# Scores of an attention block in two-half and three-half stages, with the third half in the banks of the feed-forward layer

## Chip, cores, metric

One core of one Trainium2 chip. The metric is the device time of one execution in microseconds, as the median of several; kernels are compared by the ratio of the mean time of one kernel's fast runs to that of the other's fast runs of the same rounds, so a ratio is not quite the ratio of the medians quoted beside it. TensorE is written PE in the profile, VectorE DVE, ScalarE ACT, GpSimd POOL, SyncE (which issues most transfers) SP.

## The reference

Attention with a local window of 96 keys and 8 global keys and a distance bias for each head, followed by a feed-forward layer with softplus:

```python
scores = q @ k.T / sqrt(D) - slope[h] * dist      # 4 x 8 heads, 768 rows, D = 64
a      = softmax(where(is_global | is_local, scores, -1e9))
x      = (a @ v) laid out as 3072 x 512
out    = softplus(x @ w_in) @ w_out               # 512 -> 2048 -> 512
```

## The kernel before

The rows are cut into 24 blocks of 128 (six to a batch entry), two blocks make a window, and there are 12 groups of 256 rows for the feed-forward layer. A half is four of a block's eight heads, and a stage is one run of score matmuls on TensorE. A planner inside the kernel starts each operation in a simulated order and the instructions are issued in that order, engine by engine. TensorE interleaves mm1 (x @ w_in), mm2 (softplus @ w_out), the scores and pv (a @ v).

```python
raw = tile_pool(bufs=2); qkv = tile_pool(bufs=2)           # q32, qb, qT ... two buffers each
s_ps = [psum [P, 8, P]] * 2     # one half (4 heads) of a block's scores each: two banks each
h_ps = [psum [P, 512]] * 2      # the two banks of mm1
x_ps, o_ps                      # one bank each: pv and mm2
...
def scores_both(n):             # a stage: both halves of block n
    scores(n, 0, s_ps[0], True)
    scores(n, 1, s_ps[1], True)
...
def globals_k(n):               # GpSimd: global keys over rows of the previous block's keys, in place
def globals_v(n): ...           # VectorE: the same for v
...
pl = Planner({"S0": 1, "S1": 1, "X": 1, "H": 2, "O": 1, ..., "qb": 2, "kb": 2, "qT": 2}, ...)
...
for i in range(2):              # a window's q and k are transposed by two DMAs each
    o = pl.add(f"D{what}{w}", "sp", 1.3, ..., takes=takes if i == 0 else (), ...)
...
frees_q = [(first_t[w, "q"], "qT")] if half == 1 and n % 2 == 1 else []   # after the window's last scores
```

`takes=takes if i == 0 else ()`: in the plan only the first of the two transposes has to wait for a free buffer of transposed q.

The softmax here doesn't subtract the row's maximum and nothing guards it: scores larger than these inputs give would overflow.

## Time and profile before

| | before |
|---|---|
| median of three runs | 218.81 us (218.69 to 219.37) |
| span of the profiled run | 217.1 us |
| PE, ACT, DVE, POOL busy | 97%, 72%, 53%, 28% |
| mean granted TensorE clock | 0.999 |

PE is the engine to watch: in the chain of waits it carries 86% of the span, and the other engines wait for it. The row of the page with the granted clock, in 40 slices, is 9 everywhere (9 means 90% or more):

```profile
PEclk9999999999999999999999999999999999999999
```

### The profile page before, as it was taken

To read this page: it belongs to the slowest core of one execution; us is meant where nothing else is said; L and a number is where in the kernel's file an instruction comes from. 1 tells how busy PE (TensorE), PEld (TensorE's weight loads), DVE (VectorE), ACT (ScalarE), POOL (GpSimd) and SP (SyncE) were. 2 spreads that over 40 slices of the span, in tenths; PEclk is the share of its full clock that TensorE was granted. 3 is DMA by queue.
4 is the path that set the end of the run, shared out by engine and by line. 5 is a ranking of instruction groups with operands and counts; after the bars stand their busy time and mean duration, and the time that the engine had idled before them with its cause. 6 is when DMAs were issued, how large, how long until landed. Compare 5 with 4: busy or idle time off the path is not lost.

```text
span 217.1 us, 5087 instructions
## 1 busy us (share of the span) xinstructions
PE 210.4 (97%) x2073; PEld 146.2 (67%) x2073; DVE 115.8 (53%) x247; ACT 157.1 (72%) x210; POOL 61.1 (28%) x119
## 2 busy tenths in 40 slices
PE   7799999999999999999999999999999999999993
PEld 7577775766667766667767767666766766776542
DVE  6565554728696585885544954663763663110120
ACT  4686885995969957888959669668768758857700
POOL 3770290014727170540404260331350000000000
PEclk9999999999999999999999999999999999999999
DMA  5999999999999986969866885887791211201112
GB/s 159 301 220 196 271 154 197 222 303 278 176 264 262 211 192 195 259 86 227 133 167 174 163 184 167 198 195 195 158 209 48 76 24 51 72 0 48 51 44 102
DMA packets 71511, 35.98 MB, mean 166 GB/s; under 512 B 27328, under 2 KB 68544, under 8 KB 71488
## 3 DMA queue, kind: packets, MB, share of 16 engines
q1 hardware_dynamic: 67120, 31.27, 63.0%
q0 software_dynamic: 4224, 4.19, 12.2%
q8 instruction: 16, 0.26, 0.5%
q10 hardware_dynamic: 144, 0.20, 0.2%
q14 instruction: 7, 0.06, 0.1%
HBM read 27.26 MB, written 6.29 MB: 155 GB/s over the span
## 4 chain that ended last, share of the span: by engine, by line
PE 86%; DMA 9%; POOL 2%; ACT 1%; SPq 0%; issue 0%; DVE 0%; ACTq 0%
PE h_ps L492 36%; PE o_ps L520 31%; PE s_ps L393 5%; DMA w_in_bf<-in_moe_w_in_dram 4%; PE x_ps L448 4%; PE s_ps L545 3%; DMA q<-in_q_dram 2%; DMA v<-in_v_dram 2%; PE s_ps L520 2%; PE o_ps L646 1%; PE h_ps L319 1%; PE s_ps L378 1%; POOL vb L302 1%; ACT pb L434 1%; PE h_ps L470 1%; PE x_ps L445 1%
## 5 line engine op out<-in xcount | busy, mean ns | idle before, releaser
L492 PE MATMUL h_ps<-XT,w_in_bf 128*128 128x256 bf16 x768 | 96.4, 273 | 0.5 <-DMA w_in_bf<-in_moe_w_in_dram 0.3
L492 PEld LDWEIGHTS <-w_in_bf 128*128 128x128 bf16 x768 | 73.2, 98 | 21.1 <-DMA w_in_bf<-in_moe_w_in_dram 0.8
L520 PE MATMUL o_ps<-w_out_bf,g 128*128 128x512 bf16 x320 | 82.2, 379 | 0.0
L503 ACT ACTIVATE e<-h_ps 128x512 f32<-128x512 f32 x96 | 59.2, 630 | 29.8 <-PE h_ps L492 29.5
L511 ACT ACTIVATE g<-e 128x1024 bf16<-128x1024 f32 x48 | 50.7, 1056 | 0.8
L520 PEld LDWEIGHTS <-g 128*128 128x128 bf16 x352 | 31.9, 98 | 23.8 <-issue 0.3
L430 ACT ACTIVATE pb<-z 128x1024 bf16<-128x1024 f32 (+1 forms) x40 | 39.1, 985 | 8.2 <-DVE z L424 8.0
L424 DVE TENSOR_TENSOR z<-s_ps,biasA 128x1024 f32<-128x1024 f32 x34 | 40.8, 1219 | 7.1 <-PE s_ps L393 6.5
L302 POOL CAST vb<-v 64x512 bf16<-64x512 f32 (+1 forms) x46 | 27.5, 598 | 13.2 <-DMA v<-in_v_dram 11.2
L459 DVE RECIPROCAL rcp<-x_ps 128x4 f32<-128x4 f32 x44 | 7.9, 180 | 43.0 <-PE x_ps L448 38.9
L302 POOL CAST kb<-k 64x512 bf16<-64x512 f32 x32 | 19.7, 615 | 35.8 <-DMA k<-in_k_dram 34.6
L564 DVE COPY osb<-o_ps 128x512 f32<-128x512 f32 x20 | 13.7, 686 | 25.7 <-PE o_ps L520 25.5
L460 DVE TENSOR_TENSOR xs<-x_ps,rcp 128x256 bf16<-128x256 f32 x44 | 18.7, 425 | 1.5
L448 PEld LDWEIGHTS <-pb 128*128 128x128 bf16 x320 | 14.5, 97 | 4.1
L393 PEld LDWEIGHTS <-kT 64*128 64x128 bf16 x352 | 10.0, 94 | 8.4 <-issue 7.2
L393 PE MATMUL s_ps<-qT,kT 64*128 64x128 bf16 x352 | 15.1, 218 | 0.0
L448 PE MATMUL x_ps<-vb,pb 128*128 128x65 bf16 x288 | 14.6, 193 | 0.0
L362 POOL COPY kT<-kT 128x32 bf16<-128x32 bf16 x16 | 3.3, 209 | 39.2 <-issue 19.8
L371 DVE COPY vb<-vb 4x512 bf16<-4x512 bf16 x32 | 9.9, 309 | 0.5
L293 DVE CAST qb<-q 128x1024 bf16<-128x1024 f32 x10 | 6.9, 690 | 5.2 <-DMA q<-in_q_dram 5.1
L646 PE MATMUL o_ps<-zeros 128*128 128x128 bf16 x89 | 7.8, 251 | 1.0 <-DVE zeros L599 1.0
L434 ACT ACTIVATE pb<-s_ps 128x1024 bf16<-128x1024 f32 (+1 forms) x8 | 7.3, 917 | 1.6 <-PE s_ps L393 1.6
(61 smaller groups left out, 99.3 us busy)
## 6 DMA issues: line engine op xcount, KB each, us to landing
out_dram<-osb SPq DMA_DIRECT2D x23, 256.0 KB, 2.3
q<-in_q_dram SPq DMA_DIRECT2D x11, 512.0 KB, 5.4
k<-in_k_dram SPq DMA_DIRECT2D x11, 512.0 KB, 5.8
v<-in_v_dram SPq DMA_DIRECT2D x11, 512.0 KB, 5.4
w_in_bf<-in_moe_w_in_dram POOLq DMA_DIRECT2D x4, 512.0 KB, 8.1
w_out_bf<-in_moe_w_out_dram POOLq DMA_DIRECT2D x4, 512.0 KB, 11.0
q<-in_q_dram SPq DMA_DIRECT2D x2, 256.0 KB, 4.1
k<-in_k_dram SPq DMA_DIRECT2D x2, 256.0 KB, 4.4
```

The costliest lines, as they stand in the source:

```text
L302: copy_on[eng](dst[64 * r : 64 * r + 64, hs, :], src)
L393: nc.tensor.matmul(s_t[:, 4 * sub + (lh // 2 if i == 0 else 2 * (lh // 2) + b), :], k_of(n - b, rows, m), q_of(n, rows, m), start=begin, s ...
L424: nc.vector.tensor_tensor(packed(n, z), rows_of(n, s_t), bias, ALU.add)
L430: nc.scalar.activation(pb[:, 0:nr, :], z[:, 0:nr, :], AF.Exp, scale=1.0 / root_d)
L448: nc.tensor.matmul(xv[:, lh, :], pb[:, 2 * j + b, :], vb_of(n - b)[:, h, :], start=b == 0, stop=b == 1,)
L460: nc.vector.tensor_tensor(xs[:, 4 * half : 4 * half + 4, :], xv[:, :, 0:D], rcp[:][:, :, None].to_broadcast([P, 4, D]), ALU.mult,)
L492: nc.tensor.matmul(hv[:, j, :], w_in_bf[:, m, fb * P : fb * P + P], XT[:, m, W * g : W * g + W], start=(m == 0), stop=(m == NM - 1),)
L503: nc.scalar.activation(e[:, p % 2, :].rearrange("p (a t r) -> p a r t", a=4, r=2), state["h", g, p][:].rearrange("p (a r t) -> p a r t", a ...
L511: nc.scalar.activation(gt[:, 4 * c : 4 * c + 4, :].rearrange("p a t -> p (a t)"), state["e", g, c][:].rearrange("p a t -> p (a t)"), AF.Ln ...
L520: nc.tensor.matmul(dst, state["g", g][:, fb, ns * P : ns * P + P], w_out_bf[:, fb, :], start=(fb == 0), stop=(fb == NFB - 1),)
L564: copy_on[eng](osb[:], src)
L646: nc.tensor.matmul(o_ps[:, 0:P], zeros[:], zeros[:])
```

## The change

Intent: a stage of scores has a fixed cost on TensorE (about 0.21 us in the profile of before, worked out in the prediction below), so put three halves in a stage instead of two, from block 12 on. In the program's layout no pair of banks is free for the third half, so it takes both mm1 banks while the stage lasts. Since a block's first half now runs together with the block before it, the global keys can't overwrite the older block's keys in place yet; a shifted copy (kp) is used instead.

```diff
+    def stage(items, slot, off):
+        for j, (n, half) in enumerate(items):
+            s_t = (h_ps, s_ps[0], s_ps[1])[j]
+            ...
+                    takes=(("S0",), ("S1",), ("H",), ("H",)) if j == 0 else (),
+    def attention_triple(n):
+        stage([(n, 0), (n, 1), (n + 1, 0)], ...)
+        stage([(n + 1, 1), (n + 2, 0), (n + 2, 1)], ...)
...
+    def global_keys(n, rank, half=None, copied=False):
+        ...
+        for h in range(2):
+            if half in (None, h):
+                gk[n, h] = op = pl.add(f"gk{n}", "pool", dur, fn, rank, after=after)
...
+    def copy_k(n, half):        # GpSimd: keys of the previous block to kp, global keys on top
...
+        if isinstance(s_t, list):   # bias from the two mm1 banks: two instructions
```

Uncut, it also gives the new operations tuned places (a table of offsets), offers loads of windows from 6 on earlier, and orders mm2 from group 5 on differently.

More of the change, by code (lines that the diff above doesn't have):

```diff
@@ L14 @@
 BF16 = mybir.dt.bfloat16
+OFF = (-27.07, 2.51, 30.33, 25.71, -15.87, 17.77, -14.25, 0.3, 10.38, -16.15, 14.93, 41.55,
+       10.74, -48.65, -23.68, -19.66, 40.71, 6.61, -15.76, 29.51, 1.83, 2.96, -0.96, -3.56, -12.08)
 class Op:
@@ L354, in vb_of, with globals_k @@
         return vb_ring[n // 2 % NRING][:, n % 2, :, :]
-    def globals_k(n):
+    def globals_k(n, ms=slice(0, NPAIR)):
         first = n - n % NBLK
-        kd = state["kT", (n - 1) // 2][:, (n - 1) % 2, :, :]
-        ks = state["kT", first // 2][:, 0, :, :]
+        kd = state["kT", (n - 1) // 2][:, (n - 1) % 2, ms, :]
+        ks = state["kT", first // 2][:, 0, ms, :]
         nc.gpsimd.tensor_copy(
@@ L393, in scores @@
                 nc.tensor.matmul(
-                    s_t[:, 4 * sub + (lh // 2 if i == 0 else 2 * (lh // 2) + b), :],
-                    k_of(n - b, rows, m),
+                    part_of(s_t, 4 * sub + (lh // 2 if i == 0 else 2 * (lh // 2) + b)),
+                    prev_k(n, half, rows, m) if b else k_of(n, rows, m),
                     q_of(n, rows, m),
@@ L399, in scores, with part_of, prev_k @@
                 )
+    def part_of(s_t, j):
+        if isinstance(s_t, list):
+            return s_t[j // 4][:, P * (j % 4) : P * (j % 4) + P]
+        return s_t[:, j, :]
+    def prev_k(n, half, rows, m):
+        if ("kp", n, half) in state:
+            return state["kp", n, half][rows, m - 2 * half, :]
+        return k_of(n - 1, rows, m)
+    def copy_k(n, half):
+        first = n - n % NBLK
+        kp = tile_of(work, ("kp", n, half), [P, 2, P], BF16)
+        ms = slice(2 * half, 2 * half + 2)
+        nc.gpsimd.tensor_copy(kp[:], state["kT", (n - 1) // 2][:, (n - 1) % 2, ms, :])
+        nc.gpsimd.tensor_copy(
+            kp[:].rearrange("p m (r t) -> p m r t", r=2)[:, :, :, 0:GH],
+            state["kT", first // 2][:, 0, ms, :].rearrange("p m (r t) -> p m r t", r=2)[:, :, :, 0:GH],
+        )
     def rows_of(n, t):
@@ L423, in add_bias @@
             bias = bias.rearrange("p (e j) t -> p e j t", e=2)
+        if isinstance(s_t, list):
+            nr = 2 if n % NBLK == 0 else 4
+            bias = bias0 if n % NBLK == 0 else biasA
+            for e, bank in enumerate(s_t):
+                part = slice(nr * e, nr * e + nr)
+                nc.vector.tensor_tensor(
+                    z[:, part, :], bank[:, 0 : nr * P].rearrange("p (j t) -> p j t", t=P),
+                    bias[:, half, part, :], ALU.add,
+                )
+            return
         nc.vector.tensor_tensor(packed(n, z), rows_of(n, s_t), bias, ALU.add)
@@ L659 @@
     whole = ((ALL, range(NPAIR)),)
+    TRIPLES = 12
+    LATE = 5
+    STAGES = {12: ((4, 5), (5, 2)), 15: ((6, 1), (6, 6)), 18: ((7, 5), (8, 2)), 21: ((9, 1), (9, 6))}
     POOL_ORDER = "q1 in0 in1 out0 q2 out1 in2 in3 out2 out3".split()
@@ L724 @@
     for w in range(4, NWIN):
-        load_rest(w, base(2 * w) - 13.87)
+        load_rest(w, base(2 * w) - 13.87 - (3.0 if 2 * w >= TRIPLES else 0.0))
     for gate, w, what in gates:
@@ L737, in attention_window @@
     def attention_window(w):
-        u = base(2 * w)
+        u = base(2 * w) - (3.0 if 2 * w >= TRIPLES else 0.0)
         last = 1 if w == 0 else 0
@@ L772, in attention_window @@
                         lambda op, what=what, hs=hs: cast(op.on, w, what, hs),
-                        u - (7.94 if w < T_DMA else 5.33) + 0.1 * (what == "k"),
+                        u - (7.94 if w < T_DMA else 5.33 if 2 * w < TRIPLES else OFF[24]) + 0.1 * (what == "k"),
                         after=loaded[w, what] if w else [loaded[w, what][part]],
@@ L934, in attention_block, with attention_values @@
             )
-    for w in range(NWIN):
-        attention_window(w)
-        for n in (2 * w, 2 * w + 1):
-            attention_block(n)
+    def attention_values(n, half, rank):
+        i, w = n % NBLK, n // 2
+        prev = n - 1 if i > 0 else None
+        po = pl.add(
+            f"pv{n}{half}", "pe", 0.13 if i == 0 else 0.25, lambda op: pv(n, half, x_of(op)), rank,
+            after=[exps[n, half], *v_of(w, half), gv.get(n),
+                   *(v_of(prev // 2, half) if prev is not None else ())],
+            takes=(("X",),), frees=[(exps[n, half], "pb")], behind=[pvs.get((n, 0))],
+        )
+        no = pl.add(
+            f"norm{n}{half}", "dve", 0.62, lambda op: normalize(n, half, x_of(po)), rank + 0.1,
+            after=[po], behind=[norm.get((n, 0))], takes=(("xs",),) if half == 0 else (),
+            frees=[(po, "X")],
+        )
+        pvs[n, half], norm[n, half] = po, no
+        if half:
+            xdone[n] = pl.add(
+                f"DX{n}", "sp", 1.3, lambda op: x_dma(n), base(n) - 19.37,
+                after=[norm[n, 0], no], frees=[(norm[n, 0], "xs")], dma=(32, 27), slack=1.7,
+            )
@@ new lines, in global_keys @@
+    def global_keys(n, rank, half=None, copied=False):
+        first = n - n % NBLK
+        after = [*outs[first // 2, "k", 0], *outs[(n - 1) // 2, "k", 0]]
+        if copied:
+            fn, dur = lambda op: copy_k(n, half), 0.6
+        else:
+            ms = slice(0, NPAIR) if half is None else slice(2 * half, 2 * half + 2)
+            fn, dur = lambda op: globals_k(n, ms), 0.22
+            after += [score[n - 1, h] for h in range(2) if half in (None, h)]
+        for h in range(2):
+            if half in (None, h):
+                gk[n, h] = op = pl.add(f"gk{n}", "pool", dur, fn, rank, after=after)
@@ new lines, in global_values @@
+    def global_values(n, rank):
+        gv[n] = pl.add(
+            f"gv{n}", "dve", 0.68, lambda op: globals_v(n), rank,
+            after=[pvs[n - 1, 1], *casts[n - n % NBLK >> 1, "v"]],
+        )
+    def stage(items, slot, off):
+        group = None
+        for j, (n, half) in enumerate(items):
+            i, w = n % NBLK, n // 2
+            s_t = (h_ps, s_ps[0], s_ps[1])[j]
+            after = [*outs[w, "q", 0], *outs[w, "k", 0], gk.get((n, half))]
+            if i > 0:
+                after += outs[(n - 1) // 2, "k", 0]
+            ops = [
+                pl.add(
+                    f"scores{n}{half}", "pe", (0.19 if j == 0 else 0.0) + (0.12 if i == 0 else 0.225),
+                    lambda op, n=n, half=half, s_t=s_t: scores(n, half, s_t, True),
+                    slot if j == 0 else -900.0, after=after, behind=[group],
+                    takes=(("S0",), ("S1",), ("H",), ("H",)) if j == 0 else (),
+                    frees=[(first_t[w, "q"], "qT")] if half == 1 and n % 2 == 1 else [],
+                )
+            ]
+            if j == 0:
+                head = ops[0]
+            group = score[n, half] = ops[0]
+            need.append((head, after))
+            ab = pl.add(
+                f"bias{n}{half}", "dve", (0.7 if i == 0 else 1.22) + (0.15 if j == 0 else 0.0),
+                lambda op, n=n, half=half, s_t=s_t: add_bias(n, half, s_t),
+                slot + off[j], after=[group], takes=(("z",),),
+                frees=[(head, ("H", "S0", "S1")[j])],
+            )
+            exps[n, half] = pl.add(
+                f"exp{n}{half}", "act", 0.6 if i == 0 else 1.05,
+                lambda op, n=n, half=half: expo(n, half), slot + off[3 + j],
+                after=[ab], takes=(("pb",),), frees=[(ab, "z")],
+            )
+        return head
@@ new lines, in attention_triple @@
+    def attention_triple(n):
+        (ga, pa), (gb, pb) = STAGES[n]
+        a, b = NSLOT * ga + pa, NSLOT * gb + pb
+        if n % NBLK:
+            global_keys(n, a - 4.0)
+            global_values(n, base(n - 1) + 5.38)
+            global_keys(n + 1, a - 4.0, 0, True)
+        need.clear()
+        before_mm1[ga, pa] = head = stage([(n, 0), (n, 1), (n + 1, 0)], a - 0.6, OFF[0:6])
+        wait_all(head)
+        if n % NBLK:
+            global_keys(n + 1, a + 1.0, 1)
+        global_keys(n + 2, a + 1.1, 0)
+        global_keys(n + 2, a + 1.2, 1, True)
+        attention_values(n, 0, a + OFF[12])
+        attention_values(n, 1, a + OFF[13])
+        if n % NBLK:
+            global_values(n + 1, a + OFF[18])
+        attention_values(n + 1, 0, a + OFF[14])
+        need.clear()
+        before_mm1[gb, pb] = head = stage([(n + 1, 1), (n + 2, 0), (n + 2, 1)], b - 0.6, OFF[6:12])
+        wait_all(head)
+        attention_values(n + 1, 1, b + OFF[15])
+        global_values(n + 2, b + OFF[19])
+        attention_values(n + 2, 0, b + OFF[16])
+        attention_values(n + 2, 1, b + OFF[17])
@@ new lines, in wait_all @@
+    def wait_all(head):
+        for _, ops in need:
+            for o in ops:
+                if o is not None and o is not head and o not in head.after:
+                    head.wait_for(o)
+    need, before_mm1 = [], {}
+    for w in range(NWIN):
+        if 2 * w < TRIPLES:
+            attention_window(w)
+            for n in (2 * w, 2 * w + 1):
+                attention_block(n)
+        elif 2 * w % 3 == 0:
+            attention_window(w)
+            attention_window(w + 1)
+            attention_triple(2 * w)
+            attention_window(w + 2)
+            attention_triple(2 * w + 3)
@@ L947 @@
                 after=[xdone[2 * g], xdone[2 * g + 1], landed_in[p * NS // NSLOT]],
-                takes=(("H",),),
+                behind=[before_mm1.get((g, p))], takes=(("H",),),
             )
             ex = pl.add(
-                f"sexp{g}_{p}", "act", 0.59, lambda op, g=g, p=p: softplus_exp(g, p), r + 0.5,
+                f"sexp{g}_{p}", "act", 0.59, lambda op, g=g, p=p: softplus_exp(g, p), r + (0.5 if g < LATE else OFF[20]),
                 after=[m1], takes=(("e",),) if p % 2 == 0 else (), frees=[(m1, "H")],
@@ L956 @@
                     f"sln{g}_{p // 2}", "act", 1.06,
-                    lambda op, g=g, p=p: softplus_ln(g, p // 2), r + 0.9, after=[ex, prev_ex],
+                    lambda op, g=g, p=p: softplus_ln(g, p // 2), r + (0.9 if g < LATE else OFF[21]), after=[ex, prev_ex],
                     takes=(("g",),) if p == 1 else (), frees=[(prev_ex, "e")],
@@ L969 @@
                         1000.0 + 4 * part + chunk,
-                        after=[lns[g, chunk], before],
+                        after=[lns[g, chunk]], behind=[before],
                         takes=((LAST[part][2][0],),) if chunk == 0 else (),
@@ L991 @@
                 lambda op, g=g, ns=ns, c=c: mm2_one(g, o_ps[:], ns, range(4 * c, 4 * c + 4)),
-                NSLOT * (g + 1) + p + (-2.58 if g < 4 else 0.5),
-                after=[lns[g, c], landed_out[c], mm2s.get((g, p - 1))],
+                NSLOT * (g + 1) + p + (-2.58 if g < 4 else OFF[22] if g >= LATE else 0.5),
+                after=[lns[g, c], landed_out[c], mm2s.get((g, p - 1)) if g < 3 else None],
+                behind=[mm2s.get((g, p - 1)) if g >= 3 else None],
                 takes=(("O",),) if c == 0 else (),
@@ L1003 @@
                 ),
-                r - 2.06 + 4 * ns, after=[mm2s[g, last], copies.get((g, 0))], takes=(("osb",),),
+                r - (2.06 if g < LATE else OFF[23]) + 4 * ns, after=[mm2s[g, last], copies.get((g, 0))], takes=(("osb",),),
                 frees=[(mm2s[g, 0], "S1")] * ns if g == 0 else [(mm2s[g, last - 3], "O")],
```

## The prediction

> **What bounds the kernel now.** I read the page first, then the wait table from 115 us on, then the timeline of TensorE alone, and only then the groups, for durations.
>
> ```profile
> PE 210.4 (97%) x2073; PEld 146.2 (67%) x2073; DVE 115.8 (53%) x247; ACT 157.1 (72%) x210; POOL 61.1 (28%) x119
> PE 86%; DMA 9%; POOL 2%; ACT 1%; SPq 0%; issue 0%; DVE 0%; ACTq 0%
> ```
>
> TensorE is busy 97% of the 217.1 us span and holds 86% of the chain that ended last; the DMA share lies in the first 40 us, which the change leaves alone (it starts at block 12). In the wait table other engines wait for TensorE:
>
> ```profile
> DVE rcp L459 <- PE x_ps L448: 22.7, 16, 2.2
> ACT e L503 <- PE h_ps L492: 17.8, 14, 2.2
> ...
> DVE osb L564 <- PE o_ps L520: 9.7, 4, 7.1
> ```
>
> No line has TensorE's matmuls waiting. But busy is no proof of useful streaming, so I read the starts (columns: start, length, engine, line, operation):
>
> ```profile
> 127.03 1.03 PE L520 MATMUL o_ps<-w_out_bf,g 128*128 128x512 bf16 x4
> 127.99 0.62 PE L393 MATMUL s_ps<-qT,kT 64*128 64x128 bf16 x16
> 128.54 1.05 PE L492 MATMUL h_ps<-XT,w_in_bf 128*128 128x256 bf16 x8
> 129.43 1.03 PE L520 MATMUL o_ps<-w_out_bf,g 128*128 128x512 bf16 x4
> 130.29 1.91 PE L492 MATMUL h_ps<-XT,w_in_bf 128*128 128x256 bf16 x16
> 132.04 0.41 PE L448 MATMUL x_ps<-vb,pb 128*128 128x65 bf16 x8
> 132.28 1.03 PE L520 MATMUL o_ps<-w_out_bf,g 128*128 128x512 bf16 x4
> ...
> 135.12 1.03 PE L520 MATMUL o_ps<-w_out_bf,g 128*128 128x512 bf16 x4
> 136.08 0.40 PE L393 MATMUL s_ps<-qT,kT 64*128 64x128 bf16 x8
> 136.41 0.83 PE L492 MATMUL h_ps<-XT,w_in_bf 128*128 128x256 bf16 x6
> ```
>
> Start to start: an mm2 group of four takes 0.86 (129.43 to 130.29), an mm1 group of eight 0.87 (half of 130.29 to 132.04), a pv group of eight 0.24. The exception is at scores. The mm2 group before them takes 0.96, so entering costs 0.10. Sixteen scores take 0.55 and eight take 0.33: 0.028 each and 0.10 that does not depend on the number. The mm1 group after takes 0.89 instead of 0.87, 0.01 to 0.02 more. A stage of scores therefore costs about 0.21 us however many scores are in it. The same 0.10 comes before every stage that I looked at from 60 us on, and I found no other loss on TensorE from there to the end of its work.
>
> [...] The scores use 64 rows and their neighbours 128; [...] exactly these two borders show a 0.10 gap each. [...] the trace has 0.87/8 = 109 and 0.86/4 = 215 to 216[...]. [...]
>
> ```profile
> L424 DVE TENSOR_TENSOR z<-s_ps,biasA 128x1024 f32<-128x1024 f32 x34 | 40.8, 1219 | 7.1 <-PE s_ps L393 6.5
> L424 DVE TENSOR_TENSOR z<-s_ps,bias 128x512 f32<-128x512 f32 x6 | 4.0, 687 | 1.2 <-PE s_ps L393 1.2
> L503 ACT ACTIVATE e<-h_ps 128x512 f32<-128x512 f32 x96 | 59.2, 630 | 29.8 <-PE h_ps L492 29.5
> L564 DVE COPY osb<-o_ps 128x512 f32<-128x512 f32 x20 | 13.7, 686 | 25.7 <-PE o_ps L520 25.5
> ```
>
> 1219 - 687 = 532 ns for 512 elements leaves 155 ns fixed.
>
> **The change part by part.** *Removed:* blocks 12 to 23 have 24 halves. Before, two per stage: 12 stages. After, three per stage: 8. The number of score matmuls is unchanged (so is TensorE's instruction count in the built programs). 4 stages x 0.21 = 0.83 us off TensorE, all of it on the path, as TensorE is the path.
>
> *Added on VectorE:* the first half of a stage lies in the two mm1 banks, and its bias is added in two instructions. Six full halves: 2 x 687 - 1219 = 155 ns more each; two first-block halves, 2 x 0.42 (155 + 256 x 1.04 ns) against 0.69, also 0.155. Together 8 x 0.155 = 1.2 us on an engine that is 53% busy: nothing on the path by itself.
>
> *Added on GpSimd:* in the built programs 16 in-place copies of global keys become 12 and 6 of half size, and six copies of shifted keys (128x256, and a small one on top) come in: a few us at most on an engine that is 28% busy. They let a block's scores run in the same stage as those of the block before, since the in-place overwrite no longer has to wait for these. Off the path.
>
> *Moved:* a stage now needs both mm1 banks empty, and no mm1 can follow until the bias has been added out of them. What stands between in the built order is what counts, and I went through all eight stages with these durations: VectorE and ScalarE start 0.20 after TensorE's nominal end of a group (pv 132.04 + 0.24, reciprocal at 132.48 in the timeline of VectorE); TensorE starts 0.05 after ScalarE's end (the one place that shows it, 42.26 to 42.31); back to back, ScalarE gives 0.52 per softplus exp, 0.95 per attention exp or log; VectorE 0.55 per normalization, 1.14 per whole bias, 0.61 per half.
>
> Into a stage, the last mm1 is mostly followed by 8 mm2 (1.73 us) before the scores; its exp needs 0.20 + 0.63 + 0.05 = 0.88. One stage, the second of blocks 12 to 14, has only 4 mm2 and 4 pv (1.0) and a ScalarE that has just caught up: 0 to 0.1.
> Out of a stage, a third of 24 scores is done at 0.33; both bank halves have left VectorE at about 0.33 + 0.20 + 2 x 0.65 = 1.8, against 0.79 + 1.73 = 2.5 when 8 mm2 follow: hidden. The first stages of blocks 12 and 18 have 16 scores and only 4 mm2 (0.56 + 0.86 = 1.42). Block 18's needs 0.20 + 0.20 + 0.8 = 1.2: hidden. Block 12's is behind a normalization: 0.10 + 0.55 + 0.76 + 0.05 = 1.47: 0.05 lost.
> In the second stages of blocks 15 and 21 the scores are followed at once by an mm2 that needs the single output bank, filled by the mm2 just before the scores: copy out 0.10 + 0.69 + 0.05 = 0.85 against 0.79: 0.06 lost, twice. In two places a pv follows a pv after one mm1 (0.87) where 0.20 + 0.63 + 0.05 = 0.88 is needed: 0.02 each.
> Sum of the losses that I can see: 0.2 to 0.3.
>
> Loads of later windows are offered earlier, but each still waits for mm2 of four groups before; from 120 us the DMA share is under 0.8. Reordering of the last groups (fewer mm2 left behind the last mm1, 48 instead of 64 instructions) changes no amount of work, and the last log is hidden: 0.20 + 0.52 + 1.06 + 0.05 = 1.8 against 12 x 0.216 = 2.6.
>
> Net: -0.83 + 0.2 = -0.6 us; 218.81 - 0.6 = 218.2.
>
> **Rivals.** *(a) The whole 0.83 stays*: the handovers are as short as planned and 218.0 results. For it: the order puts 1.7 us of mm2 on either side of most stages. Against: the output-bank case above, where 0.79 is simply shorter than 0.85. *(b) The bank handover eats the gain*: 0.1 to 0.2 at each of eight stages, so 218.8 or a little more. For it: ScalarE is at 72%, and after a stage three exps (2.9 us) come in a bunch, with mm1 in pairs behind them, each waiting for ScalarE. Against: in a stage period ScalarE's sum, at back-to-back spacing, leaves over a quarter free, as now (5.9 of 8.1 us between two stages). *(c) A head-of-line wait on VectorE*: the cast of q waits for its load (the trace shows it waiting 1.41 us for the last one, 4.5 us after its issue) and now stands just before work that empties a bank. In the order the cast of window 11 comes about 4 us after its load, with an output copy behind it; a load that takes 5.5 costs 0.5 to 1 us, so 218.7 to 219.2. *(d) A larger gain* would need idle or slow TensorE elsewhere after 100 us, and there is none: 217.8 at best.
>
> **Range and chances.** The three runs of before spread from 218.69 to 219.37. The central estimate is 218.2; (a) and noise carry it to 217.7, (b) and (c) to 218.9. A 2% change is 4.4 us, five times what the removed part is worth, so faster by that is out of reach; slower by that would take a stall of 0.6 us at every stage, or a late load that the wait table gives no hint of.
>
> **What would show it.** Right: eight score groups of 16 or 24 after block 12, 24 of them lasting about 0.79; the 0.10 gap before each; TensorE busy about 0.6 us less in all; gaps only where an mm2 waits for the output copy, below 0.1. Wrong: mm1 after a stage waiting on VectorE's bias by more than 0.2; scores waiting for ScalarE's exp of the last mm1; a fixed cost that grows with the three-bank stage; TensorE waiting behind a cast of q. A time under 217.7 would mean a loss in the old order that I did not see; over 219, that the handover is on the path.

## The result, and the profile after

Three fast runs of the changed kernel took 221.13, 221.84 and 221.95 us against 218.75 us (median of four) before: ratio 1.0123 (95% interval 1.0077 to 1.0168), slower, and above the range of the prediction (217.7 to 218.9). A fourth run, the profiled one, took 759.31 us with TensorE at about a quarter of its speed from start to end (start to start, a 256-column matmul took 420 ns instead of 109; the granted clock listed for it is 1.0, and its trace holds no clock record at all); it is of no use for the question. So the first thing I did was to run the changed kernel again for a profile of a fast run.

### Run after_again

Edit: none.

> The changed kernel unaltered, for a profile of a fast run (the one that came with the result ran at a TensorE clock several times lower from start to end and tells nothing). Theory H (handover): the 3.1 us are many small waits, 0.2 to 0.6 us at each of the eight stages, all with TensorE at full clock; then TensorE's groups between stages still take 0.87 and 0.86. Theory C (clock): the fast runs list a mean clock of 0.992 against 0.999 before; 0.007 x 220 = 1.6 us at half clock or equivalent 3 us of half speed, so there is ONE stretch of about 3.4 us in which mm1 takes 1.75 for eight instead of 0.87, costing about 1.7 us, and it follows a gap on TensorE; the rest, about 2 us (3.1 + 0.6 expected gain - 1.7), is that gap. Theory Q (queue): that gap is a late load or transpose of a window from 6 on, seen as scores or VectorE's cast of q waiting for a DMA. Time: 221 to 222 again, ratio 1.010 to 1.016.

Measured: 220.56 us median of six against 218.88, ratio 1.0077 (1.0037 to 1.0117); correct. Listed clocks: 0.992 in the profiled run, 0.998 or 1.0 in the other five. The 221 to 222 us that I expected were those of the first three runs, which all listed 0.992; here only one of six did. The page of the profiled run (span 219.7 us):

```profile
PE 211.2 (96%) x2073; PEld 147.5 (67%) x2073; DVE 116.6 (53%) x255; ACT 159.3 (73%) x210; POOL 65.0 (30%) x133
PEclk9999999999999999999996999999999999999999
PE 84%; DMA 9%; POOL 3%; ACT 1%; issue 1%; SPq 0%; DVE 0%; ACTq 0%
```

The busy shares hardly moved. One slice of the clock did: it fell to 6 near 118 us. The timeline of TensorE there (start, length, operation):

```profile
112.77 1.89 PE L556 MATMUL o_ps<-w_out_bf,g 128*128 128x512 bf16 x8
114.60 0.23 PE L397 MATMUL h_ps<-qT,kT 64*128 64x128 bf16 x1
116.66 0.34 PE L397 MATMUL h_ps<-qT,kT 64*128 64x128 bf16 x6 [1.83 <-POOL kT L366]
...
117.45 0.62 PE L484 MATMUL x_ps<-vb,pb 128*128 128x65 bf16 x8
117.88 3.31 PE L556 MATMUL o_ps<-w_out_bf,g 128*128 128x512 bf16 x8
121.03 0.71 PE L528 MATMUL h_ps<-XT,w_in_bf 128*128 128x256 bf16 x5
```

The first stage of block 15 starts at 114.60, stops after one matmul, and goes on at 116.66 when GpSimd has written global keys into kT. Then pv and eight mm2 run at half speed: the mm2 take 121.03 - 117.88 = 3.15 us where eight took 1.73 before. The same in the table of stretches (columns: busy time of PE, its weight loads, DVE, ACT, POOL, each with its count, then granted clock, DMA share, GB/s):

```profile
117.40:121.00 3.60, 3.60 (x19) 1.55 (x17) 3.22 (x7) 1.06 (x1) 0.28 (x2) 0.53 0.83 228
```

PE is "busy" for all of 117.4 to 121.0, at a clock of 0.53. The record of the clock has it at one half for 3.41 us of these 3.60, which is that 0.53: (3.60 - 0.5 x 3.41) / 3.60. That the listed 0.992 would be one stretch of about 3.4 us at half clock, behind a gap, was a guess of theory C until this trace showed it.

All of the loss is in this one place. From the first scores of block 8 to the last matmul, the order of work being the same in all versions of the changed kernel, the profile has 153.37 us here and 150.37 before. The version below that has neither stop nor half clock has 149.70. The difference to it, 3.67 us, is 2.06 in the scores of that stage (2.69 us from first to last start instead of 0.63) and 1.60 at half clock (1.42 in mm2, 0.18 in pv). Theory H, small waits at every stage, is out; C and Q are left to be shown.

Why did the global keys come so late? GpSimd's timeline, then that of the DMA queue on SyncE:

```profile
107.27 0.21 POOL L366 COPY kT<-kT 128x32 bf16<-128x32 bf16 x1 [0.88 <-POOL kb L306]
113.70 2.62 POOL L306 CAST vb<-v 64x512 bf16<-64x512 f32 x4 [6.22 <-DVE xs L496]
116.39 0.21 POOL L366 COPY kT<-kT 128x32 bf16<-128x32 bf16 x1
```

```profile
106.76 2.07 SPq L345 DMA_TRANSPOSE qT<-qb  x1
108.88 0.57 SPq L290 DMA_DIRECT2D v<-in_v_dram  x1
109.55 2.53 SPq L345 DMA_TRANSPOSE kT<-kb  x2
...
114.06 1.26 SPq L345 DMA_TRANSPOSE qT<-qb  x1
```

The copy at 107.27 is the one that block 15 needs. The one at 116.39 is the same copy again: the loop in `global_keys` adds one for each half although each does the whole. It stands behind four casts of v of window 8, which started at 113.70. The profile names a VectorE instruction as what they waited for, but the load of that v, issued at 108.88, landed at 113.58, 0.12 us before (in the profile of one_copy, below, the same casts are put down to that load). And the load stands behind a transpose of q of window 8 at 106.76, which has to wait until the scores of block 13, at 106.29, have read the buffer it overwrites. The other transpose of q of window 8, which block 16's scores in this same stage need, went out at 114.06 and landed at 116.57, hardly before the copy ended. In the kernel before, the same two transposes went together, long before block 16's scores at 119.89:

```profile
103.59 2.52 SPq L341 DMA_TRANSPOSE qT<-qb  x2
```

The time that this buffer of q has between its last reader (block 13) and its next one (block 16) has shrunk. Before:

```profile
92.74 0.62 PE L393 MATMUL s_ps<-qT,kT 64*128 64x128 bf16 x16
...
119.89 0.62 PE L393 MATMUL s_ps<-qT,kT 64*128 64x128 bf16 x16
```

After, block 13's last scores come first in this stage, and block 16's are in the stage at 114.60 shown above:

```profile
106.29 0.40 PE L397 MATMUL h_ps<-qT,kT 64*128 64x128 bf16 x8
```

So there are several candidates in one knot: the superfluous copy, the late load, the late transpose.

### The profile page after: what moved, and what is told of

Its sections match the earlier page's. It is cut to its first block, busy times and chain, and to the rows that moved or that the text cites.

```text
span 757.5 us, 5099 instructions
## 1 busy us (share of the span) xinstructions
PE 753.4 (99%) x2073; PEld 350.5 (46%) x2073; DVE 117.2 (15%) x255; ACT 164.3 (22%) x210; POOL 63.5 (8%) x133
## 4 chain that ended last, share of the span: by engine, by line
PE 99%; DVE 0%; issue 0%
PE h_ps L528 42%; PE o_ps L556 35%; PE s_ps L397 4%; PE x_ps L484 4%; PE s_ps L556 3%; PE s_ps L581 3%; PE o_ps L682 2%; PE s_ps L382 2%; PE h_ps L323 1%; PE h_ps L506 1%; PE h_ps L397 1%; PE x_ps L481 0%; PE o_ps L581 0%; PE o_ps L484 0%; PE o_ps L323 0%; PE o_ps L506 0%
## 5 line engine op out<-in xcount | busy, mean ns | idle before, releaser
L528 PE MATMUL h_ps<-XT,w_in_bf 128*128 128x256 bf16 x768 | 333.6, 693 | 0.0
L556 PE MATMUL o_ps<-w_out_bf,g 128*128 128x512 bf16 x320 | 277.8, 1095 | 0.0
L528 PEld LDWEIGHTS <-w_in_bf 128*128 128x128 bf16 x768 | 166.0, 219 | 166.2 <-issue 165.0
L556 PEld LDWEIGHTS <-g 128*128 128x128 bf16 x352 | 73.6, 214 | 148.0 <-issue 146.5
L484 PEld LDWEIGHTS <-pb 128*128 128x128 bf16 x320 | 40.0, 177 | 26.5 <-issue 21.0
L484 PE MATMUL x_ps<-vb,pb 128*128 128x65 bf16 x288 | 39.8, 346 | 0.0
L397 PE MATMUL s_ps<-qT,kT 64*128 64x128 bf16 x272 | 32.7, 435 | 0.0
L556 PE MATMUL s_ps<-w_out_bf,g 128*128 128x512 bf16 x32 | 28.6, 1114 | 0.0
L581 PE MATMUL s_ps<-w_out_bf,g 128*128 128x512 bf16 (+1 forms) x32 | 23.2, 992 | 0.0
L682 PEld LDWEIGHTS <-zeros 128*128 128x128 bf16 x89 | 16.9, 221 | 5.3 <-issue 3.0
```

Source lines behind the costliest of these rows:

```text
L397: nc.tensor.matmul(part_of(s_t, 4 * sub + (lh // 2 if i == 0 else 2 * (lh // 2) + b)), prev_k(n, half, rows, m) if b else k_of(n, rows, m) ...
L484: nc.tensor.matmul(xv[:, lh, :], pb[:, 2 * j + b, :], vb_of(n - b)[:, h, :], start=b == 0, stop=b == 1,)
L528: nc.tensor.matmul(hv[:, j, :], w_in_bf[:, m, fb * P : fb * P + P], XT[:, m, W * g : W * g + W], start=(m == 0), stop=(m == NM - 1),)
L556: nc.tensor.matmul(dst, state["g", g][:, fb, ns * P : ns * P + P], w_out_bf[:, fb, :], start=(fb == 0), stop=(fb == NFB - 1),)
L581: nc.tensor.matmul(bank_of(x)[:, 0 : cols.stop - cols.start], state["g", NGRP - 1][:, fb, ns * P : ns * P + P], w_out_bf[:, fb, cols], sta ...
L682: nc.tensor.matmul(o_ps[:, 0:P], zeros[:], zeros[:])
```

## The experiments

All gave correct results. The four of each of the next two batches shared a chip and the runs of before: 218.97 us (11 runs, 218.17 to 220.87) for the first batch, 218.75 us (11 runs, 218.19 to 220.40) for the second. That spread, also of before, is why effects below 0.5 us are read from the profiles and not from medians.

### Run one_copy

```diff
-        for h in range(2):
-            if half in (None, h):
-                gk[n, h] = op = pl.add(f"gk{n}", "pool", dur, fn, rank, after=after)
+        op = pl.add(f"gk{n}", "pool", dur, fn, rank, after=after)
+        for h in range(2):
+            if half in (None, h):
+                gk[n, h] = op
```

> The changed kernel with the second, identical in-place copy of global keys for blocks 15 and 21 left out (it is added once for each half although both do the whole). The order on the other four engines is unchanged. Theory G: the 2.0 us stop of TensorE inside the scores of block 15 is this second copy, which stands behind four casts of v that wait for their load; then the stop is gone, the clock stays at 0.998 or more, and the time is the one I predicted, 218.2 (ratio to before 0.996 to 0.999). Rival R: the stop has another cause, such as the key transposes of the window or the three-bank stage itself; then a stop of over 1 us stays at block 15 and the time stays at 219.8 to 222.

Measured: 220.39 us, ratio 1.0046 (0.9998 to 1.0094); clock 1.0 in all six runs. The rival was right: the stop only moved by one operand. The place on TensorE:

```profile
115.10 0.39 PE L397 MATMUL s_ps<-qT,kT 64*128 64x128 bf16 x8
116.85 0.23 PE L397 MATMUL s_ps<-qT,kT 64*128 64x128 bf16 x2 [1.35 <-DMA qT<-qb]
```

Block 15's two halves now run through, and block 16's half waits for the transposed q, landed at 116.81. The stage lasts 2.16 us from first to last start instead of 0.63: 1.53 lost. Another 0.66 us of this profile is lost at a pv at 137.65, which waited for a normalization behind a cast of q.

### Run load_first

The instruction moved is the only one that changes place.

```diff
+    early = names.index("Dq8")
+    plan.insert(names.index("loadv8"), plan.pop(early))     # behind the load of v of window 8
```

> The changed kernel with both copies kept; one DMA instruction moved: the transpose of the second half of q of window 8 goes behind the load of v of window 8 on SyncE's queue. Theory G says why the casts of v came late: that transpose waits for the buffer that the scores of block 13 read until 106.5, and the load stands behind it, issued at 108.9, landed at 113.6. Moved, the load is issued some 5 us or more earlier, the casts and the second copy end by about 112, before the scores at 114.6: no stop, 218.2, the same as with one copy. Rival R2: the load is late because of the DMA engines' own load; then it lands after 112 all the same and a stop of 1 us or more stays.

Measured: 219.45 us, ratio 1.0009 (0.9961 to 1.0057). The load goes out at 98.02 instead of 108.88 and the second copy ends by 110.2, so this part of the chain is as theory G said. But 0.65 us of stop stay, and the releaser is again the transpose of q: its second part goes out at 113.00, behind the transposes of k, a store and the transpose of x. The expected 218.2 was missed because I had taken the transpose for a bystander.

### Run both_mended

```diff
+                            behind=[outs[w, what, 0][0]] if i and what == "q" else (),
```

and the edit of one_copy.

> The changed kernel with one copy, and with the plan told that the second half's transpose of q can't go before the first half's. Both theories of one_copy and load_first agree that nothing more is gained if the stop is the only loss: 218.2, within 0.2 of one_copy. If other late loads cost something (rival R3), this is faster than one_copy by 0.3 us or more.

Measured: 218.25 us, ratio 0.9953 (0.9904 to 1.0001). The 218.2 came out, and this is faster than one_copy by far more than 0.3, but that doesn't show R3: one_copy still had its stop. The plan now issues both transposes of q together, behind the load, at 111.17 and 112.44; the second lands at 114.91 and costs 0.07 us. Waits of R3's kind do exist: in this profile two waits behind casts of q that wait for their load cost 0.33 us (a pv at 135.5) and 0.27 us (an mm2 at 151.84), and from block 8's scores to the last matmul it has 150.37 us, no less than before; one_copy has both kinds too (0.66 and 0.06 us). It is the transpose of q that decides the stop. With two buffers and the queue re-ordered the stop is all but gone, so the buffer alone doesn't make it. The next batch asks what the buffer does.

### Run three_q

```diff
-        ... "qb": 2, "kb": 2, "qT": 2},
+        ... "qb": 2, "kb": 2, "qT": 3},
+    qts = ctx.enter_context(tc.tile_pool(name="qts", bufs=3))
-        return tile_of(qkv, ("qT", w), [P, 2, NPAIR, P], BF16)
+        return tile_of(qts, ("qT", w), [P, 2, NPAIR, P], BF16)
```

> The changed kernel with a third buffer for transposed q and nothing else; the second copy of global keys is kept, and the order on TensorE, VectorE, ScalarE and GpSimd is unchanged. Theory B (buffers): what stopped TensorE at block 15 is that q of window 8 can't be transposed before block 13's last scores free one of two buffers, and that these now come at 106.5 us, 8 us before block 16's scores of the stage at 114.6, where before the change there were some 27; both the late transpose and the late load of v behind it follow. With a third buffer the transposes go about 5 us earlier: no stop at 114.6, no half clock, 218.2 to 218.5 (ratio 0.995 to 0.998). Rival: the copy on GpSimd matters by itself; then a stop of 0.5 us or more stays at block 15.

Measured: 217.88 us, ratio 0.9956 (0.9923 to 0.9989), clock 0.998 or more in all six runs. The transposes and the load:

```profile
102.28 2.51 SPq L346 DMA_TRANSPOSE qT<-qb  x2
104.83 0.58 SPq L291 DMA_DIRECT2D v<-in_v_dram  x1
```

and the stage on TensorE:

```profile
114.76 0.40 PE L398 MATMUL h_ps<-qT,kT 64*128 64x128 bf16 x8
114.99 0.45 PE L398 MATMUL s_ps<-qT,kT 64*128 64x128 bf16 x10
...
115.54 0.42 PE L485 MATMUL x_ps<-vb,pb 128*128 128x65 bf16 x8
115.79 1.89 PE L557 MATMUL o_ps<-w_out_bf,g 128*128 128x512 bf16 x8
```

Nothing waits, 24 scores take 0.78 us, and mm2 runs at full speed. The superfluous copy is still in this kernel; it ended at 114.22, half a microsecond before it was needed. Theory B stands: one more buffer of q, with the order on the four compute engines untouched, turns the loss into the gain. The third buffer let the first transpose go at 102.28, before block 13's scores at 106.45. But the order on SyncE changed with it: in the trace the planner has put the second transpose of q directly behind the first. The order alone, with two buffers and one copy, removed the stop but for 0.07 us (both_mended); the third buffer in the old order was not run.

### Run three_q_one_copy

Edit: three_q with the edits of one_copy and both_mended.

> The same with the second copy left out as well. Theory B: the copy is only a carrier of the wait, so this is within 0.2 us of three_q. Rival: 0.5 us faster.

Measured: 217.79 us, ratio 0.9953 (0.9917 to 0.9988): as theory B says. Its median is the lowest of all, but not apart from three_q's; both are below the kernel before. In its profile the distance from block 8's scores to the last matmul is 149.70 us, equal to that of three_q to 0.01.

### Runs stall_in_before and short_stall

Does the half clock belong to the three-bank stage, or to any stop? In the kernel before, the global keys of block 17 are moved behind the casts of k of window 9 on GpSimd and delayed by idle copies (ten, then eight); of the edit, the idle copies:

```diff
+            for _ in range(10):                              # 8 in short_stall
+                nc.gpsimd.tensor_copy(scratch[:], biasA[:, 0, 0:2, :]...)
```

> The kernel before, with ten idle copies on GpSimd ahead of the global keys of block 17, so that TensorE stops once, for about 2 us (10 x 0.40 + 0.21 after the casts of k end near 125.9, against scores due at 128.0), in a kernel that has none of the change. Theory C: such a stop costs more than its length, as the clock falls to half for one stretch of 3.41 us afterwards in some or all runs: 218.8 + 2.0 + 0.5 x 3.41 = 222.5 where it falls, clock 0.992 listed, and 220.8 where it doesn't. Rival: the half clock belongs to the three-bank stage and not to the stop; then 220.8 in every run and 0.998 or more.

> The kernel before with eight idle GpSimd copies instead of ten (they took 0.455 each, so ten stopped TensorE for 2.99 us and all six runs listed a clock of 0.990 to 0.992). Eight stop it for about 2.1. Theory C: the half clock follows a stop only where it is long enough; in the changed kernel 2.03 had it in the profile and 1.54 with one copy had it in no run. 2.1 should then have it in some runs and not in others: 218.9 + 2.1 = 221.0 without and 222.7 with it, clock 1.0 or 0.992. Rival: it comes with any stop at block 15 to 17; then 0.992 in every run.

Measured: 223.38 us with ten, ratio 1.0189 (1.0145 to 1.0233), clock 0.990 or 0.992 in all six runs. With eight 220.88 us, ratio 1.0113 (1.0068 to 1.0158): four runs at 0.998 to 1.0 with 220.60 to 221.04 us, and two at 0.990 and 0.991, with 222.61 and 223.17 us. TensorE's waits in the two profiles, ten copies first:

```profile
PE s_ps L393 <- POOL kT L362: 2.8, 1, 2.8
```

```profile
PE s_ps L393 <- POOL kT L362: 1.7, 1, 1.7
```

Measured from start to start, less the 0.03 us of one matmul, the stops are 2.99 (2 expected) and 1.90 us. The longer one made the distance from block 8 to the end 4.69 us longer, 3.0 of stop and 1.7 of half clock; the shorter, in a run without half clock, 1.93. The kernel before has none of the change, so the half clock belongs to the stop. The stop of 2.03 us in the changed kernel drew it in the profiled run and not in the other five of that batch; in the first batch all three fast runs listed 0.992. one_copy, with a stop of 1.54 us in its profile, had it in none of six. Only the profiled run of each has its stop measured: in short_stall that one, with 1.90 us, kept the full clock, and how long the other two stood isn't known.

Over the profiled runs, the half clock followed stops of 2.03 us (after_again), 2.8 us (cast_later, below) and 2.99 us (stall_in_before), and the clock stayed full after stops of 1.90 us (short_stall) and 1.54 us (one_copy). My estimate from these five is an edge between 1.90 and 2.03 us; no run tested it. Why the same kernel drew the half clock in some runs and not in others isn't shown.

### Run cast_later

```diff
+    moved = [op for op in plan if op.name in ("castq10", "Dq10")]   # to behind norm171
```

on top of three_q_one_copy.

> As three_q_one_copy, with the cast of q of window 10 put behind the two normalizations of block 17 on VectorE (the order elsewhere unchanged). In four profiles of changed kernels one pv at about 136 us waited 0.02 to 0.65 us for a normalization behind this cast, which waits for its load. Expected: that wait gone, 0.2 to 0.4 us on average better than three_q_one_copy: about 217.9, the best of all.

Measured: 221.01 us as the median of six, ratio 1.0064 (1.0010 to 1.0118) from five, since one run (222.35 us) counts as slow: a clear miss, as even the fastest, 218.96, is above every run of three_q_one_copy. Holding back the cast of window 10 held back the transposes and loads behind it on SyncE's queue; the q of window 11, issued at 145.02 behind two stores and a load of v, took 7.0 us to land, and VectorE's list has the cast of it ahead of an output copy:

```profile
152.12 0.69 DVE L298 CAST qb<-q 128x1024 bf16<-128x1024 f32 x1 [4.20 <-DMA q<-in_q_dram]
152.74 0.68 DVE L601 COPY osb<-o_ps 128x512 f32<-128x512 f32 x1
```

```profile
153.47 1.01 PE L557 MATMUL o_ps<-w_out_bf,g 128*128 128x512 bf16 x2 [2.61 <-DVE osb L601]
```

TensorE stopped for 2.8 us and the half clock followed, from 153.31 to 156.72: the two mm2 above took 1.01 us, where two at full clock, at 149.25, took 0.59 (three of the six runs list 0.992). This is the prediction's rival (c), at the very place that it named, but in a kernel that I had made: in the changed kernel as given, in three_q and in three_q_one_copy no such wait is in the profile, and in one_copy and both_mended it is the 0.06 and 0.27 us named above. The wait at 136 us that the edit was meant to remove (0.5 us in the wait table of one_copy, none in that of three_q) is real in some runs and was left alone.

## Why the prediction was wrong, point by point

- **What bounds the kernel, and the fixed cost of a stage: right.** TensorE holds 71 to 94% of the chain that ended last in every profile at usual speed. The 0.10 us gap stands before each of the eight stages too, and 24 scores last 0.78, as worked out.
- **The sum "-0.83 + 0.2 = -0.6": right as a sum over TensorE, VectorE and ScalarE.** From block 8's scores to the last matmul, before has 150.37 us and three_q 149.70: -0.68. The losses that I named are there: 0.04 for block 12's bias (0.05 said), 0.07 at each of the two output-bank places (0.06 said), none at block 18, and none above 0.03 where a pv follows a pv.
- **Rival (b), the bank handover: wrong, as held.** Three exps in a bunch after a stage cost nothing that a profile shows.
- **The step that failed** is the paragraph on what was moved: "What stands between in the built order is what counts, and I went through all eight stages with these durations." I went through banks, biases and exps, and for inputs wrote only that "Loads of later windows are offered earlier" and, of GpSimd's work, "Off the path." (its count of 12 in-place copies holds the two superfluous ones). I did not ask when a stage's last read frees an input buffer and when the next stage first needs that buffer. Before, block 13's scores at 92.74 freed q for window 8, first read at 119.89: 27 us. After, it is freed by scores that start at 106.29 and read at 114.60: 8 us, in which a transpose of q, a load, two transposes of k, a store, a transpose of x and another transpose of q have to pass a single queue in order. What the runs showed in place of "off the path" is a stop that cost 2.06 us, and it went when a third buffer was given, which re-ordered the queue too (three_q), and, but for 0.07 us, when the queue alone was re-ordered and the second copy left out (both_mended).
- **The clock was not in the sum at all.** I took TensorE's clock for given. In the profiled run of after_again the stop cost 2.06 us and the half clock behind it 1.60 us more (3.0 and 1.7 in stall_in_before): 2.06 + 1.60 - 0.68 = 3.0 us is what the profiled run lost.
- **The signs of being wrong.** The prediction names "a late load that the wait table gives no hint of" as what a 2% loss would take, and that was of the right kind. Its sign "over 219, that the handover is on the path" was not: the time was over 219 and no handover was on the path. The high end of 218.9 did not follow from any count of the buffers.
- **Readings that say less than was made of them.** The fixed 155 ns on VectorE is an estimate from two sizes of one operation, 1219 and 687 ns, both from PSUM. Between stages the trace has 109 and 215 to 216 ns from start to start and in before no wait of TensorE from 60 to 213 us; that a matmul can't take less was not shown. The 0.21 us of a stage is seen again in three_q, 0.10 before its first score, 0.10 after its last (the last two scores, at 0.028 us each, take 0.16 us from 115.38 to 115.54) and 0.01 in what follows, but that it comes from the change between 128 and 64 rows was not tested. 4 x 0.21 and 0.10 + 0.69 + 0.05 are both 0.84, not 0.83 and 0.85, which changes nothing.

What stays open: one run of after_again took 222.09 us at a listed clock of 1.0, more than the stop accounts for, and before itself has runs of 220 to 221 us at full clock. Only profiled runs have a trace, and none of them shows what these lost. No run takes the three-half stages without the rest of the diff (loads offered earlier, tuned places), so what share each has in the order of SyncE's queue isn't known.

## What to carry to other kernels

When a change moves the last reader of an input buffer later and its next reader earlier, write down the time between the two for every ring of buffers, not only for the banks that the change is about, and follow the in-order queue that has to refill it. A planner that lets one of two transfers into a buffer without taking it gives no warning: the wait appears on the chip, and what stands behind it in that queue waits too (the load of v went out at 108.88 us behind the waiting transpose in after_again, at 98.02 in front of it in load_first). On an engine that is otherwise dense, price a stop by more than its length: the one that cost 2.06 us in the profiled run of after_again brought 1.60 us of half clock with it, while five of that kernel's six runs drew none.
